# Retention and a quick-GELU MLP in float32 on one core: the ring's loads split in two and pinned, and the third differences of w_out traced four units later

## The chip, the cores and the metric

The kernel runs on one NeuronCore of one Trainium2 chip. The time is that of one execution on the device in microseconds (us), and the figure for a kernel is the median of its runs. A profiled execution also leaves a trace: the start and end of each instruction on each engine, and the transfers. Its span runs from the first to the last instruction of the program; its own time is a little more than the span.

## The reference

There are 4 batches, 8 heads, 768 positions and a head size of 64, all in float32. A decaying state runs along the positions, and what comes out of it goes through two matrices with a quick GELU between them.

```python
gamma = 1.0 - 2.0 ** (-5.0 - np.arange(H))
for t in range(S):                                   # per batch and head
    state = gamma * state + outer(k[t], v[t])
    y[t] = (1 / sqrt(D)) * q[t] @ state
x = y.transpose(0, 2, 1, 3).reshape(B * S, H * D)    # 3072 x 512
h = x @ w_in                                         # 512 x 2048
g = h * (1.0 / (1.0 + np.exp(-1.702 * h)))
out = g @ w_out                                      # 2048 x 512
```

## The kernel before

**Blocks.** The 3072 rows are done in six blocks `m` of 512 rows. A block is four chunks, and a chunk is 64 positions of two batches. The attention of the chunks (`step`, with `turn`, `masked`, `decay`, `output`, `aged`, `updated`) is woven into the MLP of the block before, one chunk at a time. Block 0 and block 1 have their own up projections, written out in a long list of works at the start; blocks 2 to 5 use `up(d)`. A block's up projection leaves `g` (the hidden layer after the GELU), and its down projection multiplies `g` by `w_out`.

**Seven products for eight.** Both projections use a scheme that replaces eight block products by seven, at the price of sums and differences of the blocks. The quarters of `w_out` lie in `W2[:, 0:4]`; `sums_w2` (lines 535 to 539) makes four combinations from them, and `sums_w2_t3` (line 542) makes the last one, the third difference, `W2[:, 6] = W2[:, 5] - W2[:, 0]`. For `g` of block 0, `sums_g` (lines 546 to 548) makes three combinations in place. Blocks 0 and 1 use one level of the scheme in `down(m)`; blocks 2 to 5 use two levels, 49 products, in `down49`.

**Units of block 0's down projection.** `down(0)` is a list of 28 units, four to each of the seven products. A unit is eight recorded TensorE matmuls (line 799). Units 8 to 11 are the product of the fourth quarter of `g` with `W2[:, 1]`; behind unit 8+d the kernel traces `sums_g(0, 2d)`, which overwrites the quarters of `g` that this unit has just read. Units 12 to 15 are the product of the new `a[0]` of `sums_g` with `W2[:, 5]`, so unit 12+d waits for line 548 of `sums_g(0, 2d)`. Units 20 to 23 are the product with `W2[:, 6]`: these are the first to read the third differences. Before the change `sums_w2_t3` is traced behind units 8 to 11. Behind unit 8 stands `turn(8)`, two VectorE transposes (line 253), behind unit 11 `step(8)` with its VectorE mask (line 318), and behind unit 17 `turn(9)`, two more transposes.

**The ring.** The sums of `w_out` that the second level needs were written to DRAM tiles `W2D[i]`, one per product `i` = 0 to 6, each three parts k of 128 x 512. In `down49` they come back through `ring`, an SBUF tile with two slots of three parts. `stream(ring, i)` (line 635) is the transfer of 768 KB from `W2D[i]` into slot `i % 2`, on GpSimd's queue. `begin_ring` gives those of i = 0 and 1 during the up projection. A product i is two units: half 0 with four small products, of which the last uses part k = 1 of the slot, and half 1 with three, of which the first and the third use parts k = 0 and k = 2. Behind half 1 of product i its slot is free, and the transfer for i + 2 is given.

**Output additions.** `then(i, half, p0)` takes the result out of PSUM. For i = 1, 4, 5 and 6 it calls `put`, which adds a kept product on VectorE (line 687) and, in half 1, makes four small additions (lines 692 to 695) and a DMA of 256 KB to the output (line 696). Up to block 4 the additions and the DMA are on GpSimd; in block 5 they are on VectorE and ScalarE.

**Who sets the order.** TensorE runs in the order in which the code issues its work. The other engines' instructions are ordered by a planner that simulates the program and, on each engine, takes what its simulated time has as ready, earlier traced work first. `tc.keep_in_program_order(x)` pins instruction x behind the one traced just before it on the same engine, and behind that one alone. On the chip every engine runs its list in order and waits where an operand or a buffer is missing. GpSimd (POOL in the profile) has in its list, besides ring transfers and output additions, `decay` (line 274, from the freshly loaded `kn_in`), `aged` (line 359), and `sums_x` (lines 530 to 533), which makes the combinations of x that the next block's `up` reads. SyncE (SP) issues the loads of q, k and v.

Of the kernel before, what the change touches and what calls it, by code (L numbers as in the profile page):

```python
# [28 lines left out]
def kernel(  # L29
# [29 lines left out]
    pe, act, dve, pool, sp = nc.tensor, nc.scalar, nc.vector, nc.gpsimd, nc.sync  # L59
# [13 lines left out]
    NP = NFF // 2  # L73
# [19 lines left out]
    W2D = [dram.tile([P, 3, NP // 2, P], F32, name=f"W2D{i}") for i in range(7)]  # L93
    W2 = const.tile([P, 7, NP, EH], F32, name="W2")
# [444 lines left out]
        dve.tensor_sub(w[1], w[2], w[5])  # L539

    def sums_w2_t3(p):
        dve.tensor_sub(W2[:, 6, p:p + 2, :], W2[:, 5, p:p + 2, :], W2[:, 0, p:p + 2, :])

    def sums_g(m, p):
        a = [g(m, p, s) for s in range(4)]
# [56 lines left out]
    def w2q(w):  # L602

        return [W2[:, w, u::2, e * P:(e + 1) * P] for u in range(2) for e in range(2)]
# [27 lines left out]
    def stream(ring, i):  # L632

        c = ring[:, i % 2 * 3:i % 2 * 3 + 3]
        pool.dma_start(c, W2D[i])  # L635
        return c

    def begin_ring():

        ring = late.tile([P, 7, 4, P], F32, name="ring", tag="late0")  # L640
        return ring, {i: stream(ring, i) for i in range(2)}

    def down49(m, ring, comps):

        b, t0 = m * CB // NC * 2, m * CB % NC * D
        rows = out.rearrange("(b t) (e c) -> e t b c", b=B, c=EH)[:, t0:t0 + TH, b:b + 2, :] \
            .rearrange("e (h p) b c -> h e p b c", p=P)
        own = late.tile([P, 7, 4, P], F32, name="own", tag="late1")
        acc, kept = {}, {}

        def derive(i):
            q = [G[:, u::2, ORDER[i][0], h * P:(h + 1) * P] for u in range(2) for h in range(2)]
            a11, s3, a12, s2 = q
            d = own[:, i % 2 * 3:i % 2 * 3 + 3]
            dve.tensor_add(d[:, 0], s2, a11)
            dve.tensor_sub(d[:, 1], a12, s2)
            dve.tensor_add(d[:, 2], s2, s3)
            b11, t3, b21, b22 = w2q(ORDER[i][1])
            t1, t2, t4 = [comps[i][:, k] for k in range(3)]
            return [(a11, b11), (a12, b21), (s2, t2), (s3, t3)], [(d[:, 0], t1), (d[:, 1], b22), (d[:, 2], t4)]  # L660

        def products(p0, pairs, new):
            for j in ((0, 1, 3, 2) if len(pairs) == 4 else range(len(pairs))):
                a, w = pairs[j]
                for d in range(NP // 2):
                    pe.matmul(p0[:, j, :], a[:, d], w[:, d], start=(new and j == 0 and d == 0),  # L666
                              stop=(d == NP // 2 - 1), skip_group_check=True)

        def home2(name, first, rest):
            kept[name] = first.rearrange("p (j e) -> p j e", e=P), rest[:, 0:3 * P].rearrange("p (j e) -> p j e", e=P)  # L670
            return kept[name]

        flat = X[:, 4:6].rearrange("p s c t -> p (s c t)")
        def keep(name, half):
            if half == 0:
                if name in "pt":
                    home2(name, flat[:, 0:4 * P], flat[:, 4 * P:7 * P])
                else:
                    home2(name, (own if name == "u" else ring)[:, 6].rearrange("p j e -> p (j e)"),
                          one.tile([P, 2 * EH], F32, name=name, tag="s2" if name == "u" else "s3"))  # L680
            return kept[name][half]

        def put(th, e, half, y, a):
            if half == 0:
                kept[th, e] = two.tile([P, 7, P], F32, name="o")
            c = kept[th, e]
            dve.tensor_add(c[:, 4 * half:4 + 3 * half], y, kept[a][half])
            if half == 0:
                return
            last = m == NB - 1  # L690
            eng = dve if last else pool
            eng.tensor_add(c[:, 1:3], c[:, 1:3], c[:, 0:1].to_broadcast([P, 2, P]))
            eng.tensor_add(c[:, 3], c[:, 3], c[:, 2])
            eng.tensor_add(c[:, 0:5:4], c[:, 2:4], c[:, 4:5].to_broadcast([P, 2, P]))
            eng.tensor_add(c[:, 2:4], c[:, 0:4:3], c[:, 5:7])
            (act if last else pool).dma_start(rows[th, e], c[:, 1:5].rearrange("p (b f) e -> p b (f e)", b=2))

        def then(i, half, p0):
            if i == 0:
                act.activation(keep("p", half), p0, AF.Copy)  # L700
            elif i == 1:
                put(0, 0, half, p0, "p")
            elif i == 2:
                act.activation(keep("u", half), p0, AF.Copy)
            elif i == 3:
                act.activation(keep("v", half), p0, AF.Copy)
            elif i == 4:
                u = kept["u"][half]
                dve.tensor_add(keep("t", half), p0, u)
                put(1, 1, half, p0, "v")  # L710
            elif i == 5:
                put(0, 1, half, p0, "t")
            else:
                put(1, 0, half, p0, "v")

        def finish(p0, ab):

            c, v = kept[1, 0], kept["v"][1]
            p1 = ps.tile([P, 2, P], F32, name="pq", tag="x")
            products(p0, ab[:1], True)  # L720
            products(p1, ab[1:], True)
            at = [rows[1, 0][:, b, f * P:(f + 1) * P] for b in range(2) for f in range(2)]
            dve.tensor_add(c[:, 1:3], c[:, 1:3], c[:, 0:1].to_broadcast([P, 2, P]))
            act.dma_start(at[0], c[:, 1])
            dve.tensor_add(c[:, 3], c[:, 3], c[:, 2])
            dve.tensor_add(c[:, 4], p0[:, 0], v[:, 0])
            dve.tensor_add(c[:, 0:5:4], c[:, 2:4], c[:, 4:5].to_broadcast([P, 2, P]))
            act.dma_start(at[3], c[:, 4])
            dve.tensor_add(c[:, 5:7], c[:, 0:4:3], v[:, 1:3])
            dve.tensor_add(c[:, 2:4], p1, c[:, 5:7])  # L730
            for n in range(2):
                (act, sp)[n].dma_start(at[1 + n], c[:, 2 + n])

        pairs = {}
        todo = []
        for i in range(7):
            for half in range(2):
                def unit(i=i, half=half):
                    if half == 0:
                        if i == 0:  # L740
                            pairs[0] = derive(0)
                        x = "x" if i in (0, 2, 3) else "y"
                        if i != 2 and i != 3:
                            for n in range(2):
                                acc[x, n] = ps.tile([P, 4 - n, P], F32, name="pq", tag=x)
                    x = "x" if i in (0, 2, 3) else "y"
                    if i == 6 and half == 1 and m == NB - 1:
                        finish(acc[x, half], pairs[i][half])
                        return
                    products(acc[x, half], pairs[i][half], i not in (2, 3))  # L750
                    then(i, half, acc[x, half])
                    if half == 0 and i < 6:
                        pairs[i + 1] = derive(i + 1)
                    if half == 1:
                        if i + 2 < 7:
                            comps[i + 2] = stream(ring, i + 2)
                        if i in (0, 1, 3):
                            sums_g_outer((0, 1, None, 2)[i])
                todo.append(unit)
        return todo  # L760
# [161 lines left out]
    for name, i in [("0a", 0), ("0b", 1)] + [(str(p), 2 * p) for p in range(1, NFF)]:  # L922
        n = Narrow(i)
# [42 lines left out]
    for m in range(NB):  # L966
# [8 lines left out]
        elif 1 < m < NB - 1:  # L975
            last = min((m + 2) * CB, NCH - 1)
# [4 lines left out]
        if m > 1:  # L981
# [3 lines left out]
            for d in range(NP // 2):  # L985
# [5 lines left out]
                if d == NP // 2 - 2:  # L991
                    ring = begin_ring()
# [5 lines left out]
        for n, unit in enumerate(down(m) if m < 2 else down49(m, *ring)):  # L998
            unit()
            if m == 0 and n < NP and n % 2:  # L1000
                sums_w2(n - 1)
            if m == 0 and NP <= n < 3 * NP // 2:
                sums_w2_t3(2 * (n - NP))
            if m == 1 and n % 8 == 3:
                sums_w1(n // 4)
            if (m, n) in INNER:
                inner_w2(INNER.index((m, n)))
            if between and (n in (2, 5, 11, 16, 21) if m == 1 else n % 3 == (1 if m else 2)):
                between.pop(0)()
            if 0 < m < NB - 1 and n == (23 if m == 1 else 11):  # L1010
                sums_x()
# [46 lines left out]
```

## Time and profile before

| | us |
|---|---|
| median of 3 runs (660.8 to 662.55) | 662.11 |
| profiled execution: its own time | 662.24 |
| profiled execution: span | 660.5 |
| TensorE busy (PE), share of the span | 642.2, 97% |
| VectorE busy (DVE) | 453.9, 69% |
| GpSimd busy (POOL) | 198.8, 30% |
| ScalarE busy (ACT) | 159.0, 24% |
| ring transfers: 28 of 768 KB, median from issue to landing | 4.8 |
| TensorE idle from 105 us to the end, by stage (105 to 153.5, block 0's down and block 1 to 261.5, blocks 2, 3, 4, 5) | 0.0, 1.2, 0.7, 0.7, 0.0, 3.6 |

Times in the trace are counted from the start of the span. A group of instructions is named by its line, engine and operation and by the tiles it writes and reads (`out<-in`); "idle before" is how long the engine stood idle just ahead of an instruction, with what ended that idle time. TensorE's matmuls overlap each other, so a matmul of 0.38 us may start 0.22 us after the one before it, and the distance of starts says more than the busy time. "issue" as a releaser means that the engine waited for nothing that the profile shows. The last stage's 3.6 us are the additions and transfers behind the last matmul. GpSimd's durations are rough.

### The profile page before, as it was taken

The page shows a single profiled execution, that of the slowest core. Times are in us where ns is not written, and L with a number is a line of the kernel's source. Part 1 is how long each engine was busy: PE and PEld are TensorE (multiplying, and loading weights), DVE is VectorE, ACT ScalarE, POOL GpSimd, SP SyncE. Part 2 cuts the span into 40 slices and gives each one's busy share as a digit, 9 for nine tenths or more (in the row PEclk, how much of TensorE's full clock was granted, in tenths as well). Part 3 has the DMA queues.
Part 4 walks back from the last instruction along what each step waited for, and adds up shares of the span by engine and source line. Part 5 has one row for each costly group of instructions (what it writes and reads, how often), then busy time and mean ns, then how long its engine had stood idle before and what let it go on. Part 6 is the DMA issues. An engine that isn't in the chain of part 4 may idle for free.

```text
span 660.5 us, 15291 instructions
## 1 busy us (share of the span) xinstructions
PE 642.2 (97%) x6390; PEld 580.2 (88%) x6390; DVE 453.9 (69%) x645; ACT 159.0 (24%) x306; POOL 198.8 (30%) x225
## 2 busy tenths in 40 slices
PE   6789999999999999999999999999999999999997
PEld 3778888888788888889999888999888999988997
DVE  3699989999936973556984445995354995254965
ACT  4674233551000000333100233010233110233110
POOL 6400311310379217000536400445600255500000
PEclk9989999999999999999999999999999999999999
DMA  9995549763233556262485832386742252602142
GB/s 176 193 274 173 152 104 241 172 163 60 49 82 135 137 149 153 58 248 96 118 199 134 279 57 97 86 223 135 225 118 97 66 154 104 235 21 96 55 154 96
DMA packets 148149, 91.86 MB, mean 139 GB/s; under 512 B 131600, under 2 KB 134416, under 8 KB 147056
## 3 DMA queue, kind: packets, MB, share of 16 engines
q1 hardware_dynamic: 135856, 45.19, 29.8%
q0 software_dynamic: 9888, 44.46, 20.6%
q10 hardware_dynamic: 2336, 1.25, 0.6%
q8 instruction: 50, 0.82, 0.5%
q14 instruction: 19, 0.16, 0.1%
HBM read 72.89 MB, written 15.47 MB: 134 GB/s over the span
## 4 chain that ended last, share of the span: by engine, by line
PE 89%; DVE 4%; DMA 4%; SPq 1%; issue 1%; ACT 0%; DVEq 0%
PE pq L666 27%; PE px L562 17%; PE pd L799 13%; PE py L562 13%; PE ph L491 7%; PE ph L414 5%; PE pa L289 2%; PE py L312 2%; PE pa L297 2%; PE py L306 2%; DMA W<-in_moe_w_in_dram 1%; DMA W<-in_moe_w_out_dram 1%; DMA q_in<-in_q_dram 1%; PE pt L250 1%; SPq L140 1%
## 5 line engine op out<-in xcount | busy, mean ns | idle before, releaser
L635 POOL DMA_DIRECT2D ring<-W2D x28 | 15.4, 551 | 227.7 <-PE px L562 118.3
L666 PE MATMUL pq<-W,G 128*128 128x128 f32 x672 | 80.2, 276 | 0.0
L666 PEld LDWEIGHTS pq<-W,G 128*128 128x128 f32 x672 | 77.6, 192 | 1.3 <-issue 0.7
L666 PE MATMUL pq<-ring,own 128*128 128x128 f32 x448 | 60.1, 276 | 1.3 <-issue 1.3
L562 PE MATMUL px<-X,W1A 128*128 128x256 f32 x256 | 59.8, 379 | 0.0
L562 PE MATMUL px<-X,W1B 128*128 128x256 f32 x256 | 59.8, 379 | 0.0
L666 PEld LDWEIGHTS pq<-ring,own 128*128 128x128 f32 x448 | 54.5, 192 | 0.4
L562 PEld LDWEIGHTS px<-X,W1B 128*128 128x128 f32 x256 | 48.5, 190 | 6.7
L562 PEld LDWEIGHTS px<-X,W1A 128*128 128x128 f32 x256 | 48.4, 190 | 6.5
L393 ACT ACTIVATE G<-G 128x512 f32<-128x512 f32 x60 | 37.4, 628 | 54.7 <-DVE G L572 33.4
L799 PE MATMUL pd<-W,G 128*128 128x256 f32 x224 | 49.6, 381 | 0.0
L799 PEld LDWEIGHTS pd<-W,G 128*128 128x128 f32 x224 | 42.2, 190 | 5.9
L562 PE MATMUL py<-X,W1A 128*128 128x256 f32 x192 | 45.4, 379 | 0.0
L562 PE MATMUL py<-X,W1B 128*128 128x256 f32 x192 | 45.4, 379 | 0.0
L562 PEld LDWEIGHTS py<-X,W1A 128*128 128x128 f32 x192 | 36.5, 190 | 5.0
L562 PEld LDWEIGHTS py<-X,W1B 128*128 128x128 f32 x192 | 36.5, 190 | 5.0
L580 DVE TENSOR_TENSOR t<-py,u 128x512 f32<-128x512 f32 x16 | 11.1, 692 | 32.3 <-PE py L562 32.3
L569 ACT ACTIVATE p<-px 128x512 f32<-128x512 f32 x16 | 9.6, 597 | 96.0 <-PE px L562 96.0
L414 PE MATMUL ph<-X,W1A 128*128 128x256 f32 x128 | 30.6, 397 | 0.9 <-DVE X L347 0.9
L594 DVE TENSOR_TENSOR G<-G 128x512 f32<-128x512 f32 (+2 forms) x24 | 12.3, 513 | 25.7 <-ACT G L393 25.7
L666 PE MATMUL pq<-ring,G 128*128 128x128 f32 x224 | 29.6, 275 | 0.0
L666 PE MATMUL pq<-W,own 128*128 128x128 f32 x224 | 29.6, 275 | 0.0
(237 smaller groups left out, 1226.0 us busy)
## 6 DMA issues: line engine op xcount, KB each, us to landing
ring<-W2D POOLq DMA_DIRECT2D x28, 768.0 KB, 4.8
W1B<-W1D POOLq DMA_DIRECT2D x6, 1792.0 KB, 9.8
W<-in_moe_w_in_dram SPq DMA_DIRECT2D x12, 512.0 KB, 5.9
W<-in_moe_w_out_dram SPq DMA_DIRECT2D x10, 512.0 KB, 5.8
out_dram<-o POOLq DMA_DIRECT2D x20, 256.0 KB, 3.0
q_sq<-in_q_dram SPq DMA_DIRECT2D x144, 32.0 KB, 2.1
k_sq<-in_k_dram SPq DMA_DIRECT2D x144, 32.0 KB, 2.1
v_in<-in_v_dram SPq DMA_DIRECT2D x72, 64.0 KB, 3.1
```

The lines of the kernel that those rows point to most:

```text
L289: pe.matmul(pa[HALF[w], u, 0, s, :], kt[HALF[u], w, s, :], qt[HALF[u], w, s, :], start=True, stop=True)
L297: pe.matmul(pa[HALF[u], w, 1, s, :], kd[HALF[w], HP * u + s, :], vn[HALF[w], HP * u + s, :], start=True, stop=True)
L306: pe.matmul(py[HALF[o], u, 1, 2 * w + s2, :], old[HALF[u], w, 2 * s2 + o, :], qt[HALF[u], w, 2 * s2 + o, :], start=True, stop=True)
L312: pe.matmul(py[HALF[o], w, 0, 2 * u + s2 if f < NEW else 2 * s2 + u, :], vn[HALF[w], HP * u + s, :], a[HALF[w], u, s, :], start=True, stop ...
L393: pin(act.activation(g, h[:, i], AF.Gelu_apprx_sigmoid))
L414: pe.matmul(h[:, ab], w, X[:, 2 * th + c // 2, c % 2, :], start=(ab == 0 and c == 0), stop=(c == 3), skip_group_check=True)
L491: pe.matmul(acc[:, u, :], w, x, start=(start and u == 0 and c == 0), stop=(stop and c == 1), skip_group_check=True)
L562: pe.matmul(acc[:, u, :], t[:, q1 + u, sa, c, :], X[:, sb, c, :], start=(start and u == 0 and c == 0), stop=(stop and c == 1), skip_group_ ...
L594: dve.tensor_sub(q[0][1], q[0][0], q[0][1])
L635: pool.dma_start(c, W2D[i])
L666: pe.matmul(p0[:, j, :], a[:, d], w[:, d], start=(new and j == 0 and d == 0), stop=(d == NP // 2 - 1), skip_group_check=True)
L799: pe.matmul(p0[:, n, :], g1(m, p, sa)[:, n * P:(n + 1) * P], W2[:, sb, p, :], start=(new and p == 0 and n == 0), stop=(last and p == NP - ...
```

## The change

Three things are edited.

- `sums_w2_t3` is traced behind units 12 to 15 of `down(0)` in place of units 8 to 11, and each of its four subtractions is pinned behind the VectorE instruction traced before it. The first of them then stands behind the mask of `step(8)`, the others behind one another, and the transposes of `turn(9)` behind the last.
- `stream` gives two transfers in place of one: part k = 1 (256 KB), and then parts k = 0 and 2 (512 KB). Both are pinned behind the GpSimd instruction traced before them.
- In `down49` the transfer for i + 2 is traced before `then(i, 1, ...)`, so ahead of the output additions of half 1, and not behind them. `put`'s output DMA is pinned behind the instruction traced before it on its queue.

```diff
     def sums_w2_t3(p):
-        dve.tensor_sub(W2[:, 6, p:p + 2, :], W2[:, 5, p:p + 2, :], W2[:, 0, p:p + 2, :])
+        tc.keep_in_program_order(dve.tensor_sub(W2[:, 6, p:p + 2, :], W2[:, 5, p:p + 2, :], W2[:, 0, p:p + 2, :]))
...
         c = ring[:, i % 2 * 3:i % 2 * 3 + 3]
-        pool.dma_start(c, W2D[i])
+        for k in (slice(1, 2), slice(0, 3, 2)):
+            tc.keep_in_program_order(pool.dma_start(c[:, k], W2D[i][:, k]))
         return c
...
-            (act if last else pool).dma_start(rows[th, e], c[:, 1:5].rearrange("p (b f) e -> p b (f e)", b=2))
+            tc.keep_in_program_order((act if last else pool).dma_start(
+                rows[th, e], c[:, 1:5].rearrange("p (b f) e -> p b (f e)", b=2)))
...
                     products(acc[x, half], pairs[i][half], i not in (2, 3))
+                    if half == 1 and i + 2 < 7:
+                        comps[i + 2] = stream(ring, i + 2)
                     then(i, half, acc[x, half])
                     if half == 0 and i < 6:
                         pairs[i + 1] = derive(i + 1)
                     if half == 1:
-                        if i + 2 < 7:
-                            comps[i + 2] = stream(ring, i + 2)
                         if i in (0, 1, 3):
                             sums_g_outer((0, 1, None, 2)[i])
...
             if m == 0 and n < NP and n % 2:
                 sums_w2(n - 1)
-            if m == 0 and NP <= n < 3 * NP // 2:
-                sums_w2_t3(2 * (n - NP))
+            if m == 0 and 3 * NP // 2 <= n < 2 * NP:
+                sums_w2_t3(2 * n - 3 * NP)
```

## The prediction

> **What bounds the kernel now.** I read the page's busy shares first, then TensorE's waits, then the timeline where waits show, then GpSimd's timeline around the ring.
>
> ```profile
> PE 642.2 (97%) x6390; PEld 580.2 (88%) x6390; DVE 453.9 (69%) x645; ACT 159.0 (24%) x306; POOL 198.8 (30%) x225
> ```
> ```profile
> PE pq L666 <- issue: 1.3, 2, 0.7
> PE pd L799 <- DVE W1B L548: 1.2, 2, 0.9
> ```
>
> TensorE is busy 97% of the span, and from 105 us to its last matmul (2.5 us of waits) there is nothing else to win than these two rows: two in blocks 2 and 3 that no releaser explains, and two waits in block 0's down projection for `sums_g`. No row has TensorE waiting for the ring. The second row's place on the timeline, VectorE then TensorE then GpSimd:
>
> ```profile
> 167.26 0.68 DVE L542 TENSOR_TENSOR W<-W 128x512 f32<-128x512 f32 x1
> ...
> 169.66 1.27 DVE L542 TENSOR_TENSOR W<-W 128x512 f32<-128x512 f32 x2
> 170.85 0.68 DVE L546 TENSOR_TENSOR X<-W1A,X 128x512 f32<-128x512 f32 x1
> 171.45 0.68 DVE L542 TENSOR_TENSOR W<-W 128x512 f32<-128x512 f32 x1
> ...
> 174.46 1.76 DVE L546 TENSOR_TENSOR X<-W1B,X 128x512 f32<-128x512 f32 x1
> ...
> 180.83 1.15 DVE L548 TENSOR_TENSOR W1B<-g,W1B 128x512 f32<-128x512 f32 x1
> ```
> ```profile
> 175.00 3.88 PE L799 MATMUL pd<-W,W1A 128*128 128x256 f32 x16
> 179.76 1.99 PE L799 MATMUL pd<-W,W1B 128*128 128x256 f32 x8 [0.89 <-DVE W1B L548]
> 182.04 1.13 PE L799 MATMUL pd<-W,W1B 128*128 128x256 f32 x4 [0.28 <-DVE W1B L548]
> ```
> ```profile
> 174.10 1.58 POOL L552 TENSOR_TENSOR W1A<-W1A 128x512 f32<-128x512 f32 x1 [3.28 <-DVE W1A L548]
> ```
>
> The reader is to see three third differences (L542) standing between the end of unit 8 and the second line of `sums_g`, and TensorE's units 14 and 15 starting late. A unit of eight takes 1.73 us in flow (64 matmuls in 13.83 us on the chain of work). Units 12, 14 and 15 start at 175.00, 179.76 and 182.04; in flow 14 and 15 would start at 178.46 and 180.19. So the stall at unit 15 is 182.04 - 180.19 = **1.85 us**, more than the 1.2 of the waits view, since restarts count too. That is the most the moved differences can give.
>
> For the ring, GpSimd's list around product i = 1 of block 2, TensorE's first use of that transfer, and the block's end:
>
> ```profile
> 324.42 1.64 POOL L692 TENSOR_TENSOR o<-o 128x256 f32<-128x256 f32 x1 [3.08 <-DVE o L687]
> 326.14 0.78 POOL L693 TENSOR_TENSOR o<-o 128x128 f32<-128x128 f32 x1
> 326.87 0.58 POOL L635 DMA_DIRECT2D ring<-W2D  x1
> ```
> ```profile
> 335.11 1.06 PE L666 MATMUL pq<-ring,G 128*128 128x128 f32 x8
> ```
> ```profile
> 459.33 1.04 POOL L274 TENSOR_TENSOR kd<-kn_in,cold 128x512 f32<-128x512 f32 x1 [4.39 <-DMA kn_in<-in_k_dram]
> ...
> 466.53 1.27 POOL L532 TENSOR_TENSOR X<-X 128x512 f32<-128x512 f32 x1
> ```
> ```profile
> 468.04 1.24 PE L562 MATMUL px<-X,W1A 128*128 128x256 f32 x5
> ```
>
> The transfer of 326.87 lands 4.7 us later, at 331.6, and is first read at 335.11: 3.5 us to spare, the tightest I found. The last two fences show the other place that matters: GpSimd waits for `kn_in`, then works in one row until `sums_x` line 532 ends at 467.80, and the matmul that reads this sum starts at 468.04: **0.24 us to spare**. At the end of block 2 the same pair is 365.59 and 366.16, 0.57 to spare; at the end of block 4 it is 564.52 against about 568.3.
>
> **What the Trainium skill says.** (1) "SBUF — State Buffer", section "SBUF: two separate sides": GpSimd and VectorE share a port pair, an exclusive lock; a VectorE operation with two SBUF inputs waits until a GpSimd operation that reads SBUF is done. The trace agrees: the L546 begun at 174.46 during GpSimd's L552 (174.10 to 175.68) takes 1.76 us in place of 0.68 and ends 0.54 after it. (2) "DMA: Bandwidth & Descriptors", section "Issuing engines are not separate DMA queues": transfers from all queues share 16 engines and interleave. The trace agrees: q loads issued between 326 and 330 land after 4.5 to 4.9 us while a ring transfer runs, those at 278 to 282 after 1.8 to 2.1. (3) The same page, "Anatomy of one DMA": about 2.0 us fixed per transfer, the rest by bytes at 436 GB/s. That gives an estimate of 3.8 us for 768 KB (measured 4.8), 3.2 for 512 KB and 2.6 for 256 KB (the output's, 3.0).
>
> **The change part by part.**
>
> *Third differences.* Ahead of the first L546 two of them go, 0.6 us each by start distance (169.66 to 170.85 is 1.19); behind it one more goes, 0.60. The chain of twelve `sums_g` lines can thus run up to 1.8 us sooner. It does not keep all of it: each L548 sets off an L552 on GpSimd, 1.58 us, and a `sums_g` line that begins in it ends 0.54 after it. Walking the same order without the differences: L546 at 169.5 (unit 8's last matmul ends at 169.3), the first L548 at about 171.6, L552s at about 172.5, 175.3 and 178.2, the last L548 caught by the third and ending at about 180.4. Unit 15 then starts at about 180.5, 1.5 sooner. If the planner runs each triple to its end, the last L548 ends between 180.5 and 181.1: 0.8 to 1.4 sooner. I take **1.3**; bounds 0.8 and 1.85. Nothing downstream should hold it back: behind unit 15 TensorE has no wait until 353 us, and SyncE's loads of the later blocks are set off by work that follows TensorE (the load at 319.95 by `kd`).
>
> *Where they go.* Behind the mask of `step(8)` VectorE has `turn(9)` and is then idle for 7.85 us, until 191.04. The four cost 4 x 0.6 = 2.4 us there; GpSimd's L524 operations from 181.4 on can stretch each to about 1.75, 7 us. Unit 20 needs the first at about 189 (190.7 before, less the gain), unit 23 the last at 194; it would be ready by 188. So 0. The transposes of `turn(9)` and SyncE's 16 loads behind them come up to 5.5 us later; next in SyncE's list is the first `W2D` store, for which SyncE waits until 195.0. It comes up to 3 us later, which the next stores' waits partly absorb; block 1's `sums_g` has over 4 us before its unit 12. Also 0.
>
> *Two transfers for one.* A transfer of 128 pieces costs GpSimd 0.55 us to issue, one of 2 x 128 pieces 0.77 (L696); the second part has that form. So 0.55 becomes 1.32: 28 x 0.77 = 21.6 us more of GpSimd's time. It is hidden in the 227.7 us for which GpSimd waits ahead of ring transfers, in block 2's end in the 3.60 us ahead of `kd` and in block 3's in 4.39. Uncovered it would be 0.8 us a transfer. TensorE gets one wait more per product, ahead of half 1, on data landed microseconds before: 0, at most 28 x 0.05 = 1.4 by the length of semaphore waits on GpSimd's queue.
>
> *Given earlier.* Part k = 1 is free once half 0 is done, so it can go at about 321.5 in place of 326.87. The rest is free only behind half 1, and by then the first two additions are done (324.42, 326.14): it goes where the transfer goes now. TensorE gains 0, since it waits for no ring transfer. The output DMA depends on the addition ahead of it anyway; its pin costs 0. The loads of q, k and v meet ring packets somewhat earlier; `kn_in` at a block's end could come a little sooner (no gain) or later. With 0.24 and 0.57 us to spare I charge **0.2** for that, bounds 0 and 1.5.
>
> Sum, against the profiled execution: 662.24 - 1.3 + 0.2 = 661.1, its span 660.5 - 1.1 = 659.4. The median is 0.13 below the profiled execution: **661.0**.
>
> **Rivals.** (a) *Absorbed.* TensorE comes 1.1 us sooner but `kn_in` and `sums_x` do not, because loads on a busy queue keep their pace; blocks 3 and 4 then wait 0.5 to 0.9 and the time is about 662. For: SyncE issues without a break from 320 us on. Against: that run starts from TensorE's work. The change not doing what it says belongs here: the planner may put the differences among the `sums_g` lines again, behind the mask, and the gain is nil. (b) *Slower: the block's end on GpSimd.* With more transfers in its simulated list the planner puts `kd` ahead of output additions that now run before it. They then stand behind the wait for `kn_in`. L694 to L696 of one output tile are 348.84 to 351.74, 2.9 us; `sums_x` is late by that less 0.57 and 0.24 in blocks 2 and 3: +5.0 in all, less the gain, about 665.9. It decides from a lateness of 1.0 us in both blocks. Against: those additions are traced ahead of `kd`. (c) *More.* The two unexplained stalls, 0.82 us each by the distance of matmul starts, move off with the shifted instruction stream: 1.3 + 1.6 less 0.2, about 659.4. Nothing in the profile ties them to the change.
>
> **How the numbers follow.** Chances: forecast 0.60 (its own range 660.2 to 661.8), (a) 0.15, (b) 0.17 (662.6 to 668), (c) 0.08. The range 659.7 to 663.8 leaves out the better part of (b) and half of (c). A measurement of this kernel can tell about 0.3%, 2.0 us, from no change, so the limits are 660.1 and 664.1. Faster: (c) and a tail of the forecast, 0.15. Slower: most of (b), 0.16. Same: 0.69.
>
> **What would show it.** Right: no L542 between the L546s, unit 15 less than 6.0 us behind unit 12's start (7.04 now), TensorE's wait for L548 below 0.5 us, and 56 ring transfers with GpSimd's L635 near 37 us. Wrong: L542 still ahead of an L548; a new wait of TensorE for `X` (L532, L533) at the start of blocks 3 to 5, or for the ring; `kd` ahead of L694 at a block's end.

## The result, and the profile after

The changed kernel takes 665.3 us (median of 9 runs, 663.85 to 666.8); the kernel before, run between them on the same chip, takes 661.67 (9 runs, 657.44 to 663.03). The ratio is 1.0064, with a 95% interval of 1.0044 to 1.0085: **slower by 0.6%**, where 661.0, a difference too small to be told from none, had been forecast. The profiled execution of the changed kernel took 663.92, its span is 662.2.

The busy shares of the changed kernel (busy us, share of the span, instructions), and its row for ring transfers (busy us, mean ns, idle time before them):

```profile
PE 641.8 (97%) x6390; PEld 579.9 (88%) x6390; DVE 457.6 (69%) x645; ACT 159.0 (24%) x306; POOL 219.9 (33%) x253
...
L636 POOL DMA_DIRECT2D ring<-W2D x56 | 35.8, 641 | 222.4 <-PE px L562 118.3
```

GpSimd is busy 21.1 us more, of which the ring transfers are 20.4 (35.8 against 15.4); VectorE is busy 3.7 us more, although it has the same 645 instructions. So some of its instructions got longer. TensorE's waits (us in total, times, longest) in the changed kernel:

```profile
PE pd L801 <- DVE W1B L548: 4.2, 1, 4.2
```

The wait for line 548, which was to go below 0.5 us, has grown from 1.2 us in two pieces to 4.2 in one. VectorE's timeline of the changed kernel around it (start, duration, line, output and inputs):

```profile
172.71 0.69 DVE L546 TENSOR_TENSOR X<-W1B,X 128x512 f32<-128x512 f32 x1
173.43 1.64 DVE L547 TENSOR_TENSOR W1B<-W1B 128x512 f32<-128x512 f32 x1
174.99 0.68 DVE L318 TENSOR_TENSOR at<-pa,mask 128x512 f32<-128x512 f32 x1
...
176.19 0.68 DVE L546 TENSOR_TENSOR g<-W1B,g 128x512 f32<-128x512 f32 x1
176.80 1.75 DVE L542 TENSOR_TENSOR W<-W 128x512 f32<-128x512 f32 x1
178.47 1.75 DVE L547 TENSOR_TENSOR W1B<-W1B 128x512 f32<-128x512 f32 x1
180.14 1.74 DVE L542 TENSOR_TENSOR W<-W 128x512 f32<-128x512 f32 x1
181.81 0.68 DVE L548 TENSOR_TENSOR W1B<-g,W1B 128x512 f32<-128x512 f32 x1
```

GpSimd's timeline of the changed kernel, in the same stretch:

```profile
172.94 1.58 POOL L552 TENSOR_TENSOR W1A<-W1A 128x512 f32<-128x512 f32 x1 [2.15 <-DVE W1A L548]
176.42 1.58 POOL L552 TENSOR_TENSOR W1B<-W1B 128x512 f32<-128x512 f32 x1 [1.90 <-DVE W1B L548]
177.96 3.37 POOL L524 TENSOR_TENSOR W1A<-W1A 128x512 f32<-128x512 f32 x2
```

And TensorE's, where the pieces of eight and sixteen are units 12 and 13, 14, 15:

```profile
172.92 3.72 PE L801 MATMUL pd<-W,W1A 128*128 128x256 f32 x16
176.48 1.89 PE L801 MATMUL pd<-W,W1B 128*128 128x256 f32 x8
182.54 3.09 PE L801 MATMUL pd<-W,W1B 128*128 128x256 f32 x8 [4.17 <-DVE W1B L548]
```

Three things are to be seen. Two third differences (L542) still stand ahead of the last L548, which is the prediction's own first sign of being wrong, now between the dependent lines of the last `sums_g`; the mask (L318), behind which the first is pinned, stands two lines of `sums_g` ahead of them. The L542 begun at 176.80 falls into GpSimd's L552 (176.42 to 178.00) and takes 1.75 us; the L547 and the L542 behind it fall into GpSimd's two L524 and take 1.75 and 1.74. And unit 15 starts 9.62 us behind unit 12, where less than 6.0 was forecast and 7.04 was measured before.

The fourth sign is that unit 15, once started, is slow: its eight matmuls take 3.09 us against 1.89 for unit 14. The busy time by stretches of the changed kernel (columns: stretch, its length, busy us of TensorE, its weight loads, VectorE, ScalarE and GpSimd, then the granted clock, the share of DMA and GB/s):

```profile
176.80:182.50 5.70, 1.57 (x8) 1.04 (x6) 5.70 (x6) 0.00 (x0) 4.54 (x3) 1.00 0.18 28
182.50:186.80 4.30, 4.26 (x12) 3.47 (x13) 3.47 (x4) 0.60 (x1) 4.24 (x3) 0.60 0.04 7
```

The granted clock is 0.60 on the mean of the second stretch. In the trace it is a stretch of 3.41 us at half speed, in which matmuls start 0.427 us apart instead of 0.216.

**The measure used below.** From the first matmul of block 0's down projection to the end of its unit 19 (five products of four units) TensorE takes 35.52 us where it doesn't wait; behind that, everything up to block 2 took the same 70.42 us in every profile that had no stall of its own there. I call the first part the stretch. It was 37.38 in the profile of before and is 41.64 in that of after. The 6.12 us over 35.52 add up: unit 15 starts 6.06 behind unit 14 instead of 1.73 (4.33), the pipeline's restart costs 0.10, and eight matmul starts at half speed cost 8 x 0.211 = 1.69; together 6.12.

### The profile page after: what moved, and what is told of

Same layout as the page of the kernel before. It is cut to its first block, busy times and chain, and to the rows that moved or that the text cites. A ratio compares the mean times of both kernels' runs of the same rounds, so it can differ in the third digit from the quotient of the medians.

```text
span 662.2 us, 15350 instructions
## 1 busy us (share of the span) xinstructions
PE 641.8 (97%) x6390; PEld 579.9 (88%) x6390; DVE 457.6 (69%) x645; ACT 159.0 (24%) x306; POOL 219.9 (33%) x253
## 4 chain that ended last, share of the span: by engine, by line
PE 86%; DMA 5%; DVE 4%; SPq 2%; issue 1%; POOL 1%; ACT 0%; DVEq 0%; POOLq 0%; ACTq 0%
PE pq L667 24%; PE px L562 16%; PE pd L801 13%; PE py L562 12%; PE ph L414 7%; PE ph L491 7%; DMA W<-in_moe_w_in_dram 2%; DMA G<-in_moe_w_in_dram 2%; PE pa L289 2%; PE py L312 1%; PE py L306 1%; PE pa L297 1%; SPq L140 1%; SPq L157 1%; DMA k_sq<-in_k_dram 1%
## 5 line engine op out<-in xcount | busy, mean ns | idle before, releaser
L636 POOL DMA_DIRECT2D ring<-W2D x56 | 35.8, 641 | 222.4 <-PE px L562 118.3
L414 PE MATMUL ph<-X,W1A 128*128 128x256 f32 x128 | 29.0, 382 | 1.3 <-DVE X L347 0.8
```

The source lines that it names most:

```text
L414: pe.matmul(h[:, ab], w, X[:, 2 * th + c // 2, c % 2, :], start=(ab == 0 and c == 0), stop=(c == 3), skip_group_check=True)
L636: tc.keep_in_program_order(pool.dma_start(c[:, k], W2D[i][:, k]))
```

## The experiments

| kernel | median us | beside it, before | ratio, 95% | the stretch, us |
|---|---|---|---|---|
| changed | 665.3 | 661.67 | 1.0064 [1.0044, 1.0085] | 41.64 |
| changed, again | 664.67 | 659.02 | 1.0074 [1.0040, 1.0107] | 41.64 |
| third differences alone | 665.45 | 659.46 | 1.0099 [1.0074, 1.0125] | 42.56 |
| ring part alone | 660.11 | 659.46 | 1.0005 [0.9983, 1.0026] | 35.52 |
| changed, GpSimd's L552 reversed in blocks 0 and 1 | 662.68 | 659.46 | 1.0058 [1.0036, 1.0081] | 35.62 |
| before, the same reversal | 662.67 | 659.46 | 1.0044 [1.0026, 1.0063] | 35.52 |
| changed, reversed in block 0 alone | 658.76 | 659.44 | 0.9995 [0.9980, 1.0010] | 35.62 |
| before, reversed in block 0 alone | 659.5 | 659.44 | 0.9997 [0.9983, 1.0012] | 35.52 |
| changed, differences behind unit 17 | 661.31 | 659.44 | 1.0027 [1.0015, 1.0039] | 39.39 |
| changed, TensorE kept busy in the wait | 663.44 | 659.44 | 1.0063 [1.0041, 1.0086] | 39.97 |
| before, three single executions | 658.26, 662.87, 659.43 | | | 35.52, 37.34, 35.52 |

**Which half of the change.** Each half alone. The first kernel has only the edit of `sums_w2_t3`, the second only those of `stream`, `put` and `down49`:

```diff
-        dve.tensor_sub(W2[:, 6, p:p + 2, :], W2[:, 5, p:p + 2, :], W2[:, 0, p:p + 2, :])
+        tc.keep_in_program_order(dve.tensor_sub(W2[:, 6, p:p + 2, :], W2[:, 5, p:p + 2, :], W2[:, 0, p:p + 2, :]))
-            if m == 0 and NP <= n < 3 * NP // 2:
-                sums_w2_t3(2 * (n - NP))
+            if m == 0 and 3 * NP // 2 <= n < 2 * NP:
+                sums_w2_t3(2 * n - 3 * NP)
```

> The third differences alone are moved and pinned as in the change; the ring and the output additions are as before. Theory A (the differences now stand between the last lines of sums_g): the same single wait for L548 as in the changed kernel, 4 to 5 us in front of unit 15, then about 3.4 us at half clock; 4.3 us slower than before, ratio 1.005 to 1.008. Theory B (the ring's 28 additional transfers and GpSimd's 21 us cost it): no wait of this size, and 0 to 1.8 us faster than before.

> The ring's transfers in two parts, earlier in the trace order and pinned, and the pinned output transfers alone; the third differences are as before. Theory A: no difference from before, within 1 us, with the two waits for L548 of 1.2 us together. Theory B: 3 to 5 us slower than before, with waits for X, for the ring or for additions in blocks 2 to 5.

The differences alone cost 1.0% and bring back the whole wait, 4.2 us for L548, with the same sequence on VectorE and a half-speed piece of 6.83 us. In its profile TensorE also waits 1.4 us for `X` from L532.

The ring part alone makes no difference that these runs can tell, and its profile has no wait for L548 at all, where the two of before had been expected (why is seen further down). So the loss belongs to the third differences. That they alone cost more than the whole change isn't settled: the intervals overlap, and the wait for `X` is discussed below. In the stretch, their 0.92 us more come from the half-speed piece, which began at 181.56, while TensorE still waited, and lasted until 188.39, twice as long.

**Is it the hold by GpSimd?** To take GpSimd's operations out of the way without moving anything on VectorE, the order of `sums_g_late` (L552) is reversed: the first of them then waits for the last L548, so none runs during `sums_g`. It computes the same. First in the changed kernel and in the kernel before, in both blocks that use this function:

```diff
-                    for p in range(0, NP, 2):
+                    for p in range(NP - 2, -1, -2):
                         sums_g_late(m, p)
```

> The changed kernel, with GpSimd's four late subtractions of block 0 (L552) in the reverse order of p. The first of them then needs the last line of sums_g, so that no GpSimd operation runs while sums_g runs; VectorE's order is that of the changed kernel, differences between the lines of sums_g included. Theory A1 (each difference is dear because it starts inside a GpSimd operation and is held until that ends, 1.75 us in place of 0.6): the wait in front of unit 15 falls to under 0.5 us, no half clock, 5 to 6 us faster than the changed kernel and 1 to 1.8 us faster than before. Theory A2 (their place in the order is enough, held or not): the wait stays above 2 us and the time near the changed kernel's.

> The kernel before, with GpSimd's four late subtractions of block 0 in the reverse order of p and nothing else. Three lines of sums_g were held there by GpSimd, for 1.08, 1.07 and 0.47 us. Theory A1: no held line, no wait for L548, 1.85 us faster than before (ratio about 0.997). Theory A2 (the differences that stand ahead of sums_g make that wait, not GpSimd): 0.2 to 0.5 us faster at most, waits for L548 still there.

Block 0's wait went in both (stretches of 35.62 and 35.52), but both kernels were slower than before. The edit reached into block 1 too, where TensorE then waited for the reversed L552 itself, 2.2 us in the one (with a half-speed piece behind it) and 1.9 in the other; from the end of the stretch to block 2 they took 4.11 and 2.13 us longer. So the two ratios say nothing on the question, and the edit was cut down to block 0:

```diff
-                    for p in range(0, NP, 2):
+                    for p in range(0, NP, 2) if m else range(NP - 2, -1, -2):
                         sums_g_late(m, p)
```

> The changed kernel with GpSimd's late subtractions (L552) in the reverse order of p in block 0 alone; block 1 keeps its order, which the earlier reversal had disturbed there (a new wait of 2.2 us for L552). Theory A1 (held differences, then the half clock): no wait for L548, none for L552, no half clock in block 0's down projection; 6 us faster than the changed kernel and 1 to 2 us faster than before. Theory A2 (their place in the order is enough): not faster than before.

> The kernel before with the same reversal in block 0 alone. Theory A1: no wait for L548, 1 to 1.85 us faster than before, if before has that wait in most of its executions; near nothing, if before has it only in some (the ring-only kernel, with VectorE's order of before, showed no such wait). Waits for X of up to 1.8 us at the start of blocks 3 and 4 may come and go, as in the last runs.

The changed kernel with this one edit is level with before, 0.9995. The expected 1 to 2 us under before do not show; 1 us would still lie in the interval. VectorE's timeline of it, from the first difference to the last L548:

```profile
175.53 0.68 DVE L542 TENSOR_TENSOR W<-W 128x512 f32<-128x512 f32 x1
176.13 0.69 DVE L547 TENSOR_TENSOR W1B<-W1B 128x512 f32<-128x512 f32 x1
176.73 0.69 DVE L542 TENSOR_TENSOR W<-W 128x512 f32<-128x512 f32 x1
177.33 0.69 DVE L548 TENSOR_TENSOR W1B<-g,W1B 128x512 f32<-128x512 f32 x1
```

GpSimd's first L552 of it, and TensorE's units 14 and 15:

```profile
178.18 3.41 POOL L552 TENSOR_TENSOR W1B<-W1B 128x512 f32<-128x512 f32 x2 [10.97 <-DVE W1B L548]
```
```profile
176.35 3.72 PE L801 MATMUL pd<-W,W1B 128*128 128x256 f32 x16
```

The order is that of the changed kernel, differences in the same gaps, and each line takes 0.68 or 0.69 us. TensorE goes from unit 14 to 15 without a break. This shows that the hold by GpSimd is the cause of the wait, and that the two differences cost nothing by where they stand as long as nothing holds them. The kernel before gains nothing from the same edit that could be measured (0.9997, where its executions with a stall could have given back 1.86).

**Are the differences needed for it?** All four are moved further back, behind unit 17 and the transposes of `turn(9)`:

```diff
-            if m == 0 and 3 * NP // 2 <= n < 2 * NP:
-                sums_w2_t3(2 * n - 3 * NP)
...
+            if m == 0 and n == 2 * NP + 1:
+                for p in range(0, NP, 2):
+                    sums_w2_t3(p)
```

> The changed kernel with the four third differences traced behind unit 17, so behind the transposes of turn(9). VectorE's order differs from the changed kernel's in one thing: between the last lines of sums_g stand the two transposes, which have one SBUF input, and not two of the differences, which have two. Theory A1 (held by GpSimd): the wait in front of unit 15 falls from 4.2 us to about 2, without the half clock (4.3 us less than the changed kernel in all, as before or up to 1 us slower). Theory A2 (an instruction in between is enough): the wait stays within 1 us of 4.2.

It is slower than before by 0.27%, less than the changed kernel. VectorE's timeline of it:

```profile
176.26 0.70 DVE L253 STREAM_TRANSPOSE qT<-q_sq 128x512 f32<-128x512 f32 x1
176.89 1.13 DVE L547 TENSOR_TENSOR W1B<-W1B 128x512 f32<-128x512 f32 x1
177.95 0.70 DVE L253 STREAM_TRANSPOSE kT<-k_sq 128x512 f32<-128x512 f32 x1
178.57 1.12 DVE L548 TENSOR_TENSOR W1B<-g,W1B 128x512 f32<-128x512 f32 x1
```

The planner filled the same gaps with the transposes, which have one input and are not held (0.70 us). L547 and L548 are held, for less long since they begin later in GpSimd's operation. TensorE waits 1.9 us, as expected, and then again runs at half speed (a mean granted clock of 0.65 from 179.70 to 184.60), which was not expected. So with no difference near it, the new order of `sums_g` still loses 3.87 us against an undisturbed stretch: the fillers are part of the loss, not its root.

**Is the half clock the idle time's doing?** Between units 14 and 15 five matmuls with `ident` (ten records) into a PSUM tile that nobody reads keep TensorE busy through most of the wait; they add work that no output depends on.

```diff
+            if m == 0 and n == 2 * NP - 2:
+                fill = ps_a.tile([P, 2, 2, 4, D], F32, name="py", tag="py")
+                for _ in range(5):
+                    pe.matmul(fill[:, 0]..., ident, ident[:, None, :].to_broadcast([P, 4, P]), start=True, stop=True)
```

> The changed kernel with five matmuls of 128x512 on the identity between units 14 and 15, into a PSUM tile that nothing reads; they fill TensorE's wait of 4.2 us (0.86 us each at full clock). Theory A (idling brought the half clock): no half clock behind unit 15, which starts within 0.2 us of where it did, counted from unit 14; 1.7 us faster than the changed kernel. If the half clock had another cause, the time stays or rises.

TensorE's timeline of it, and its stretches by clock:

```profile
178.67 4.46 PE L1007 MATMUL py<-ident 128*128 128x512 f32 x10
183.01 2.00 PE L801 MATMUL pd<-W,W1B 128*128 128x256 f32 x8
```
```profile
176.80:182.50 5.70, 5.70 (x19) 3.38 (x18) 5.70 (x5) 0.00 (x0) 4.93 (x3) 1.00 0.22 33
182.50:186.80 4.30, 4.30 (x20) 3.35 (x19) 3.95 (x5) 0.60 (x1) 3.77 (x3) 1.00 0.00 0
```

Unit 15 is as late as in the changed kernel, but runs at full clock, and the stretch is 1.68 us shorter, against the 1.69 worked out above. The half clock is in all three profiles with the empty wait of 4.2 us and not in this one, so I take it for the idle time's doing. The ratio, 1.0063, can't confirm so small a saving: the intervals reach 1.4 to 2.2 us to either side.

The length of the wait alone doesn't decide on the half clock: a wait of 1.9 us brought it with the differences behind unit 17, and another of 1.9 us did not in the kernel before, reversed in blocks 0 and 1. It is where the wait lies. In each profile the granted clock changes only on a grid of steps of 3.41 us. Two such steps with the differences behind unit 17, then two of the kernel before, reversed in blocks 0 and 1 (columns as above):

```profile
177.64:181.06 3.42, 1.51 (x7) 1.18 (x7) 3.42 (x4) 0.00 (x0) 3.42 (x3) 1.00 0.43 67
181.06:184.47 3.41, 3.41 (x10) 2.70 (x9) 3.41 (x3) 0.60 (x1) 3.41 (x3) 0.50 0.44 68
```
```profile
249.43:252.85 3.42, 2.50 (x12) 1.86 (x10) 1.21 (x3) 0.60 (x1) 3.42 (x4) 1.00 0.91 300
252.85:256.26 3.41, 2.47 (x11) 2.20 (x12) 1.09 (x2) 0.00 (x0) 3.41 (x4) 1.00 0.47 79
```

In the first pair the whole wait falls into one step, in which TensorE is busy for 1.51 us, and the next step is at half speed. In the second pair a boundary splits the wait (2.50 and 2.47 us busy), and no half speed follows. Over all fourteen profiles, from start to end, every full-speed step with TensorE busy for 1.58 us or less was followed by half speed, and none with 1.62 us or more was.

**How firm are the two kernels themselves?** The kernel before, three times by itself, and the changed kernel once more beside it, all without an edit.

> The kernel before once more, for its profile. From the first matmul of block 0's down projection to the end of unit 19 its first profile took 37.39 us, with two waits for L548; the ring-only kernel, with the same VectorE order there, took 35.53 and had none, because GpSimd's first L552 did not get the shared port. Theory C (a race for the port, one way or the other): each further profile of before shows about 35.5 or about 37.4 and nothing in between. Theory D (the ring's edit took the wait away): all of them show about 37.4.

> The kernel before once more, as in the last: about 35.5 or about 37.4 us for theory C, about 37.4 for theory D.

> The kernel before a third time: about 35.5 or about 37.4 us for theory C, about 37.4 for theory D.

> The changed kernel itself, timed and profiled again. Theory C: its dependent lines of sums_g leave VectorE a moment between any two, so that GpSimd gets the port each time: 41 to 42.5 us for the same stretch in this profile too, with the wait of about 4.2 us and the half clock; 4 to 7 us slower than before, ratio 1.006 to 1.010. If it were a race as in before, a profile with about 36 would be seen.

The changed kernel repeats itself (1.0074, the same stretch to 0.01 us, the same 4.2 us of wait). The kernel before does not. In the second repetition it is the one that the prediction read; in the first and third TensorE doesn't wait at all, with every instruction in the same order. VectorE's timeline of the first repetition, then of the second:

```profile
171.79 0.68 DVE L547 TENSOR_TENSOR W1A<-W1A 128x512 f32<-128x512 f32 x1
172.40 0.68 DVE L546 TENSOR_TENSOR X<-W1B,X 128x512 f32<-128x512 f32 x1
```
```profile
174.35 0.68 DVE L547 TENSOR_TENSOR W1A<-W1A 128x512 f32<-128x512 f32 x1
174.96 1.76 DVE L546 TENSOR_TENSOR X<-W1B,X 128x512 f32<-128x512 f32 x1
```

GpSimd's in the first repetition, with the statistics of its L552 there (least, median and most ns), then in the second:

```profile
172.03 6.87 POOL L552 TENSOR_TENSOR W1A<-W1A 128x512 f32<-128x512 f32 x2 [3.29 <-DVE W1A L548]
```
```profile
L552 POOL TENSOR_TENSOR W1A<-W1A x2: 1722/3456/5190, 172.0 to 177.2; 128x512 f32<-128x512 f32 x2
```
```profile
174.59 1.58 POOL L552 TENSOR_TENSOR W1A<-W1A 128x512 f32<-128x512 f32 x1 [3.29 <-DVE W1A L548]
```

In both, GpSimd's L552 is released in the middle of an L547. In the second it runs at once (1.58 us) and holds the L546 that begins in it. In the first it is the loser: VectorE's lines go on, 0.60 apart, and L552 takes 5.19 us. It is a race, and VectorE lost it in two of four profiles of before (and not in that of the ring part alone, which has the same order). In the changed order VectorE lost it in all five profiles that have it with GpSimd's operations in place (the changed kernel twice, the differences alone, those behind unit 17, the filled one).

Why VectorE lost each time in the new order stays open. In before, a `sums_g` line and the next one on the queue belong to different p, and they start 0.60 us apart. In the changed kernel each `sums_g` finishes before the next begins, dependent lines stand side by side, and they start 0.72 or 0.73 apart (172.71 and 173.43 above). That this longer distance lets GpSimd in is a guess, and it doesn't cover the L552 that matters: the one at 176.42 came in between an L546 and an L542 that start 0.61 apart (176.19 and 176.80), and it did so in all four profiles that have this L542 there and GpSimd's operations in place. In before's second repetition, too, it came in between lines 0.61 apart. That the triples close up follows from the pins: in before the unpinned L542 of p was traced between L548 of p and L546 of p + 2, so for p = 2 and 4 the next L546 hung on an instruction that could move ahead, and the triples could interlace. With L542 gone, this L546 hangs on the L548 before it.

## Why the prediction was wrong, step by step

**What bounds the kernel.** Right as read: TensorE is the bound, and the wait at unit 15 was real. But this wait stood in only two of the four profiles of before. If those four are typical, what could be won was nearer to 0.9 us on the mean than to 1.85, even with everything else as thought.

**Third differences: "Walking the same order without the differences" failed.** The L546 of the first `sums_g` did come sooner (15.74 us behind the start of block 0's down projection, 17.29 before: 1.55 sooner). But the order behind it was not the same. The step took the order of before and struck out the L542; the pins make another order from it. The step even named this case ("if the planner runs each triple to its end") and gave it a gain of 0.8 to 1.4, but it did not see that differences could stand among the last lines, nor that GpSimd's L524 would follow its L552 without a break (177.96) and hold one line after another. Instead of a gain of 1.3 there is a loss of 4.33 at unit 15 against an undisturbed stretch. Where it arises is seen beside the kernel that has the same order and no hold (reversed in block 0 alone). There the last L548 begins 4.54 us behind the start of unit 12 (177.33 - 172.79), in the changed kernel 8.89 (181.81 - 172.92): 4.35 later. Four held lines, by the distance of starts, make 4.17 of it: the L547 at 173.43 (1.56 for 0.60), and three at 1.67 for 0.60 (176.80, 178.47, 180.14). The other 0.18 had arisen before 172.71.

**"Where they go" failed with it.** The 1.75 us for a held difference was the right size, and it was put in the wrong place. "Behind the mask" was taken to be behind the last `sums_g` line. The profile of before already had the mask ahead of the last L548 (180.83); it could have been read there:

```profile
180.23 0.68 DVE L318 TENSOR_TENSOR at<-pa,mask 128x512 f32<-128x512 f32 x1
```

A pin behind the mask orders the difference against the mask alone. Rival (a) had said that the planner may put the differences among the `sums_g` lines, behind the mask, and that is what it did; its price, "the gain is nil", left out a loss of 4 to 6 us, because the lines there were priced at 0.6 each and not as operations with two inputs that begin in GpSimd's.

**The missing term.** The half clock behind the wait, 1.69 us, was in no case at all. It is what makes a wait of 4.2 cost 6.1.

The sum with the measured terms: against an undisturbed execution of before, 4.33 + 0.10 + 1.69 = 6.1 us; against one with the stall, 41.64 - 37.38 = 4.3. The measured ratios, 1.0064 and 1.0074, are 4.2 and 4.9 us of 660, which fits before being a mixture of the two.

**The ring.** "Two transfers for one" was right: L636 takes 35.8 us (37 forecast), 20.4 more than before (21.6 forecast), and TensorE waits for no ring transfer. The parts were slower to land than estimated, 4.5 us for 512 KB (3.2) and 3.4 for 256 KB (2.6), which cost nothing here. "Given earlier" was charged 0.2 for `kn_in` and `sums_x`. In both profiles of the changed kernel a matmul at the start of block 3 does come 0.2 us late behind a weight load that waits for `X` from L532; in the profile of before none does. Over all runs the trace points the other way: TensorE's list of waits has `X` from L532 for matmuls in six of the seven profiles without the split (0.3 to 1.4 us) and in one of the seven with it (0.7). In time, the ring part alone gives 1.0005 [0.9983, 1.0026]; whether it is worth a few tenths of a us stays open.

**The other rivals.** (b) did not come: in the changed kernel L274 (`kd`, 359.94) still stands behind the additions of the tile traced ahead of it. That its figure, about 665.9, lies so near to the measured 665.3 is chance: another mechanism brought it. (c) did not come either; the stalls without a releaser are 0.28 and 0.50 us in the changed kernel, 0.82 each in before, and up to 1.2 elsewhere. They differ between executions of before itself (0.28 at most in its first repetition), so the difference can't be put down to the change.

The Trainium skill, "SBUF — State Buffer", section "SBUF: two separate sides", says of the shared port pair that whoever starts first has it for a whole instruction and the loser is blocked entirely. The traces agree for both sides: VectorE's lines at 1.75 us instead of 0.68, GpSimd's L552 at 5.19 instead of 1.26. It was blocked for longer than one instruction, though: for 5.19 - 1.26 = 3.93 us, which is the rest of an L547 and six lines more. The prediction used the first half of that sentence and not the second, under which the stall of before is an accident of timing. On the clock, "TensorE: Matmul & The Clock Gate", section "Part 1: The HAM clock gate", speaks of half speed behind at least one idle window of about 3.4 us. The half-speed pieces here are indeed 3.41 us long (or 6.83), but waits of 1.9 us (differences behind unit 17) and 2.2 us (block 1, reversed) brought them too, while another wait of 1.9 (before, reversed) did not; here the measurement decides: a step of 3.41 us with TensorE idle for 1.91 us of it was enough.

## What to carry to other kernels

A pin orders an instruction against one other instruction only, and a line that is removed from between pinned lines changes what the next of them hangs on: write the new order out before pricing it. Where VectorE operations with two SBUF inputs run beside GpSimd's, price each by what may hold it and by what GpSimd does next, and take several profiles of the kernel before, since the stall to be won may be there only in some executions. A wait of TensorE of about 2 us or more (1.9 was the shortest here) can cost another 1.7 us in clock.

## What was not expected of the hardware

- The same instructions in the same order give two outcomes at the port: in two of four profiles of before VectorE's lines were held (1.75 us each), in the other two GpSimd's L552 was (5.19 us, where it takes 1.26 undisturbed), and the stretch was 1.86 us shorter (35.52 against 37.38).
- Past the start of the kernel the half clock came behind waits of TensorE of 1.9, 2.2 and 4.2 us, always in pieces of 3.41 us or twice that, and with the wait filled it was gone. The clock changed only on a grid of 3.41 us, and in every profile a full-speed step with TensorE busy for 1.58 us or less was followed by half speed, and none with 1.62 us or more was; so a wait of 1.9 us within one step brought it, and one that was split between two did not.
